# Spectral layers of a fused kernel: a second width sum built from the first, even wave numbers over d by parity, and another order of the row blocks

## The chip, the cores and the metric

The kernel runs on one core of a Trainium2 chip. Its engines are TensorE (PE in the profile, with its weight loads as PEld), VectorE (DVE), ScalarE (ACT), GpSimd (POOL) and SyncE (SP, which issues DMAs). The metric is the device time of one execution in microseconds (us); of several runs the median is given.

## The reference, cut to what matters

Two kinds of layer alternate: A (spectral filter), B (attention with 32 query heads and one key head), A, B. Sequence length is 2048, width 512, data bf16.

```python
def _A_ref(x, w_r, w_i):
    X = rfft2(x.astype(float32), axes=(-2, -1))
    return irfft2(X * (w_r + 1j * w_i), s=(S, D), axes=(-2, -1)).astype(bfloat16)

def _B_ref(x, wq, wk, wv, wo):
    q = (x @ wq).reshape(B, S, H, Dh).transpose(0, 2, 1, 3)
    k, v = x @ wk, x @ wv
    p = softmax(einsum("bhqd,bkd->bhqk", q, k) * Dh ** -0.5)
    return einsum("bhqk,bkd->bhqd", p, v).transpose(0, 2, 1, 3).reshape(B, S, H * Dh) @ wo

x = A_x
for _ in range(2):
    x = x + _A_ref(_layernorm(x), A_w_r, A_w_i)
    x = x + _B_ref(_layernorm(x), B_wq, B_wk, B_wv, B_wo)
```

## The kernel before, in words

The program is a loop over two pairs (L1010), each a spectral layer followed by an attention layer. The residual x stays in on-chip memory all the time as `x_sb`: 128 partitions, 4 row groups r, 4 blocks t, 512 columns. Transforms are matrix products with tables of sines and cosines. Sums over the sequence are split by parity into even wave numbers (block 0 of `Y`, `X4`, `SD`, `G`) and odd ones (block 1).

A spectral layer has three stages.

- **Front** (`front_first` L826, `front_next` L880): normalises the rows, forms sums and differences of rows (`butterfly` L156), and starts the sums over the sequence (`odd_sums`, matmuls at L202).
- **Middle** (`middle` L928): finishes those sums (`odd_sums`, `even_sums` L224), each followed by copies from PSUM to `Y` (`odd_out` L215, L228). `over_width` (L230) forms the product with the tables F2 over the width: for each of two real/imaginary parts, and for each part two results (index i) that differ in the sign of the sine term, 8 matmuls of 128x512 into one PSUM tile of two banks (L240, L241) and a copy by ACT (L242). `edge_sums` (L244) forms a few single columns. `filtered` (L254) multiplies by the filter `wt` and adds and subtracts on DVE (L267 and L270 for the products, L272 to L276). `over_d` (L282) transforms back over the width with table I1: 8 matmuls of 128x512 for each of 4 chunks kc (L292), and a copy by ACT to `G` (L293). `halves` (L295) adds and subtracts halves of the odd `G` on DVE (L300). In the first pair two casts of the query weights (`queries_cast` L924, copy at L925) stand in ACT's order here.
- **Blocks** (`blocks` L957): for each of the 4 blocks t, the inverse transform over the sequence, `odd(t)` (L308, copied by ACT to `bp` at L313) and `even(t, i)` (L324), both on PE. `rows_out(t)` (L326) adds and subtracts the two on DVE (L331, L332) into a tile `y` and adds `y` to the residual (L333, one operation of 128x2048). Then the next layer norm: statistics on DVE (L104, L105), a root on ACT (L108), scales on DVE (L112, L113), the rows normalised by ACT and DVE in turn (L128, L130), transposed by PE (L377), copied by ACT (L383; the last by DVE, L381), and projected to keys and values (L391, L393, L397, L400). `key_bound` (L403) reduces the keys on DVE; `first_queries` (L347) and `first_queries_cast` (L352, L356) prepare the first head group. The attention stage starts with the first score matmul (L538).

The order on PE, ACT and DVE is the order of the calls in the source: a manual schedule (L1032) keeps it, and the pools add semaphore waits where a buffer is used again. In the spectral stage the PSUM pool has three tiles of two banks (`big`, L186) and two of one bank (`bank`, L190). The tag `x4` has three buffers, `m` three, `big` in on-chip memory four. In the attention stage, which the diff leaves alone, a planner's lists fix the order; GpSimd works there on 128x512 tiles (L680) and on the normalisation of heads (L572). F2 and the other tables are loaded by SP's queue while the front runs.

Of the kernel before, what the change touches and what calls it, by code (L numbers as in the profile page):

```python
# [12 lines left out]
P = 128  # L13
# [26 lines left out]
def host_tables():  # L40
# [14 lines left out]
        f1[:, t, 4] = -f1[:, t, 3]  # L55
    tabs["F1"] = bf(f1)
    fs = (2 * p + 2, 2 * p + 1)
    f2 = np.zeros((P, 3, 2, 2, P))
    for fc in range(2):
        for c in range(2):  # L60
            a = 2 * np.pi * np.multiply.outer(128 * c + p, fs[fc]) / D
            f2[:, 0, fc, c], f2[:, 1, fc, c], f2[:, 2, fc, c] = np.cos(a), np.sin(a), -np.sin(a)
    tabs["F2"] = bf(f2)
    i1 = np.zeros((P, 3, 2, D))
    for fc in range(2):
# [88 lines left out]


def butterfly(nc, work, X, Z, bufs=3):  # L156
    s = work.tile([P, 4, 512], BF, tag="m" if bufs > 1 else "bs", bufs=bufs)
    e = work.tile([P, 4, 512], BF, tag="m" if bufs > 1 else "be", bufs=bufs)
    tt = nc.vector.tensor_tensor
    tt(out=s[:, 0:2, :], in0=X[:, 0:2, :], in1=X[:, 2:4, :], op=ALU.add)  # L160
    tt(out=e[:, 2:4, :], in0=X[:, 0:2, :], in1=X[:, 2:4, :], op=ALU.subtract)
    yield
    tt(out=e[:, 0, :], in0=s[:, 0, :], in1=s[:, 1, :], op=ALU.add)
    tt(out=e[:, 1, :], in0=s[:, 0, :], in1=s[:, 1, :], op=ALU.subtract)
    yield
    tt(out=Z[:, :, LO], in0=e[:, :, LO], in1=e[:, :, HI], op=ALU.add)  # L166
    yield
    tt(out=Z[:, :, HI], in0=e[:, :, LO], in1=e[:, :, HI], op=ALU.subtract)
    yield
# [7 lines left out]
class Spectral:  # L177


    def __init__(self, nc, tabs, work, small, psum, Z, Y, wt, w8, x_sb):  # L180
        self.nc, self.tabs, self.work, self.small, self.psum = nc, tabs, work, small, psum
        self.Z, self.Y, self.wt, self.w8, self.x_sb = Z, Y, wt, w8, x_sb
        self.pair, self.left, self.X4, self.SD, self.G, self.H, self.bp, self.pw = {}, {}, {}, {}, {}, None, {}, {}
        self.mm, self.tt = nc.tensor.matmul, nc.vector.tensor_tensor

    def big(self):  # L186
# [41 lines left out]
            self.nc.scalar.copy(out=self.Y[0][:, dc, :, 256 * q:256 * q + 256], in_=ps.rearrange("d (c k) -> d c k", c=2))  # L228

    def over_width(self, blk, fc):  # L230
        F2 = self.tabs["F2"]
        x_new = self.work.tile([P, 4, 512], BF, tag="x4", bufs=3)
        self.X4[(blk, fc)] = x_new
        for part in range(2):
            ps = self.big()
            for c in range(2):
                yr, yb = self.Y[blk][:, 2 * fc + c, 0, :], self.Y[blk][:, 2 * fc + c, 1, :]
                a, b = (yr, yb) if part == 0 else (yb, yr)
                for i, sg in enumerate((2, 1) if part == 0 else (1, 2)):
                    self.mm(ps[:, i, :], lhsT=F2[:, 0, fc, c, :], rhs=a, start=(c == 0), stop=False)  # L240
                    self.mm(ps[:, i, :], lhsT=F2[:, sg, fc, c, :], rhs=b, start=False, stop=(c == 1))  # L241
            self.nc.scalar.copy(out=x_new[:, 2 * part:2 * part + 2, :], in_=ps)  # L242

    def edge_sums(self, fc):  # L244
        F2 = self.tabs["F2"]
        pt = self.psum.tile([P, 8], F32, tag="mm", bufs=2)
        for i, (tab, q) in enumerate(((0, 0), (1, 0), (1, 1), (0, 1), (1, 0), (0, 0), (0, 1), (1, 1))):
            for c in range(2):
                self.mm(pt[:, i:i + 1], lhsT=F2[:, tab, fc, c, :], rhs=self.Y[0][:, 2 * fc + c, q, 0:1], start=(c == 0), stop=(c == 1))
        pw = self.work.tile([P, 8], F32, tag="pw", bufs=2)  # L250
        self.pw[fc] = pw
        self.tt(out=pw, in0=pt, in1=self.w8[:, fc, :], op=ALU.mult)

    def filtered(self, blk, fc):  # L254
        tt, work, wt = self.tt, self.work, self.wt
        if fc == 0:
            SD_new = work.tile([P, 2, 4, 512], BF, tag="big", bufs=4)
            self.SD[blk] = SD_new
        sd, x = self.SD[blk][:, fc, :, :], self.X4.pop((blk, fc))
        m1 = work.tile([P, 4, 512], BF, tag="m", bufs=3)  # L260
        m2 = work.tile([P, 4, 512], BF, tag="m", bufs=3)
        two = lambda a: a.rearrange("f (u v) k -> f u (v k)", u=2)
        w2 = lambda q: wt[:, fc, blk, q:q + 2, :].rearrange("f v k -> f (v k)")
        if blk == 1:
            for u in range(2):
                for m, q in ((m1, 0), (m2, 2)):
                    tt(out=two(m)[:, u, :], in0=two(x)[:, u, :], in1=w2(q), op=ALU.mult)  # L267
        else:
            for m, q in ((m1, 0), (m2, 2)):
                tt(out=two(m), in0=two(x), in1=w2(q).unsqueeze(1).broadcast_to([P, 2, 1024]), op=ALU.mult)  # L270
        uv = work.tile([P, 4, 512], BF, tag="m", bufs=3)
        tt(out=uv[:, 0:2, :], in0=m1[:, 0:2, :], in1=m2[:, 2:4, :], op=ALU.add)  # L272
        tt(out=uv[:, 2:4, :], in0=m1[:, 2:4, :], in1=m2[:, 0:2, :], op=ALU.subtract)
        u, v = (uv.rearrange("f (c w) k -> f c w k", w=2)[:, :, w, :] for w in range(2))
        tt(out=sd[:, 0:2, :], in0=u, in1=v, op=ALU.add)
        tt(out=sd[:, 2:4, :], in0=v, in1=u, op=ALU.subtract)  # L276
        if blk == 0:
            pw = self.pw.pop(fc)
            for i, slot in enumerate((0, 3, 2, 1)):
                tt(out=sd[:, slot, 0:1], in0=pw[:, i:i + 1], in1=pw[:, 4 + i:5 + i], op=ALU.add)  # L280

    def over_d(self, blk):  # L282
        I1 = self.tabs["I1"]
        G_new = self.work.tile([P, 4, 2, 512], BF, tag="big", bufs=4)
        self.G[blk] = G_new
        for kc in range(4):
            ks = slice(kc * P, (kc + 1) * P)
            ps = self.big()
            for i, terms in enumerate((((0, 0), (3, 2)), ((2, 1), (1, 0)))):
                for fc in range(2):  # L290
                    for n, (sd, tab) in enumerate(terms):
                        self.mm(ps[:, i, :], lhsT=self.SD[blk][:, fc, sd, ks], rhs=I1[:, tab, fc, :], start=(fc == 0 and n == 0), stop=(fc == 1 and n == 1))  # L292
            self.nc.scalar.copy(out=G_new[:, kc, :, :], in_=ps)  # L293

    def halves(self):  # L295

# [26 lines left out]
                tab = IE[:, 0, 2 * c + ab, t, :] if c < 2 else IE[:, 1, turned(c - 2, t, ab, i), t, :]  # L323
                self.mm(ps[:, i, :], lhsT=tab, rhs=self.G[0][:, c, ab, :], start=(c == 0 and ab == 0), stop=(c == 3 and ab == 1))  # L324

    def rows_out(self, t, parts=(slice(0, 2),)):  # L326
        ps, bp, x = self.pair.pop(t), self.bp.pop(t), self.x_sb[:, :, t, :]
        y = self.work.tile([P, 4, 512], BF, tag="m", bufs=3)
        two = y.rearrange("p (u i) d -> p u i d", u=2)
        for i in parts:  # L330
            self.tt(out=two[:, 0, i, :], in0=ps[:, i, :], in1=bp[:, i, :], op=ALU.add)  # L331
            self.tt(out=two[:, 1, i, :], in0=ps[:, i, :], in1=bp[:, i, :], op=ALU.subtract)  # L332
        self.tt(out=x, in0=y, in1=x, op=ALU.add)  # L333


class Attention:
# [18 lines left out]
    def qabs(self, qt):  # L355
        self.nc.vector.tensor_scalar(out=qt.bitcast(I16), in0=qt.bitcast(I16), scalar1=self.tabs["QAND"][:, 0:1], scalar2=None,  # L356
                                     op0=ALU.bitwise_and)
        return qt

    def stats(self, t):  # L360
        for r in range(R):
            self.norm.stats(self.x_sb[:, r, t, :], r, t)

    def scaled(self, work, t, engines):
        xn = work.tile([P, 4, 512], BF, tag="x4", bufs=3)
# [375 lines left out]
def full_kernel(ctx, tc, A_x, A_w_r, A_w_i, B_x, B_wq, B_wk, B_wv, B_wo, out, n_pairs=2):  # L741
# [186 lines left out]
    def middle(sp, first, wq_raw):  # L928
# [1 line left out]
        for dc in range(2):  # L930
            sp.odd_out(dc, (nc.scalar, nc.vector))
        sp.odd_out(2, (nc.scalar,))
        sp.over_width(1, 0)
        sp.filtered(1, 0)
        sp.odd_sums(3, range(T) if first else (T - 1,))
        sp.odd_out(3, (nc.scalar, nc.scalar))
        sp.over_width(1, 1)
        sp.filtered(1, 1)
        for dc in range(2):
            sp.even_sums(dc)  # L940
        if first:
            queries_cast(wq_raw, 0)
        sp.over_width(0, 0)
        sp.edge_sums(0)
        for dc in range(2, 4):
            sp.even_sums(dc)
        sp.filtered(0, 0)
        if first:
            queries_cast(wq_raw, 1)
        sp.over_width(0, 1)  # L950
        sp.edge_sums(1)
        sp.over_d(1)
        sp.filtered(0, 1)
        sp.halves()
        sp.over_d(0)

    def blocks(work, sp, psum, att):  # L957
# [8 lines left out]
                sp.even(t, i)  # L966

        def rows_ready(t):
            att.stats(t)
            norm.root(t)  # L970

        sp.odd(0)
        sums(0)
        sp.rows_out(0, (slice(0, 1), slice(1, 2)))
        sp.odd(1)
        sums(1)
        rows_ready(0)
        sp.odd(2)
        sums(2)
        xn = rows_scaled(0, both)  # L980
        sp.rows_out(1)
        att.transposed(psum, 0, xn)
        att.keys(psum, 0)
        rows_ready(1)
        att.key_bound(0)
        xn = rows_scaled(1, both)
        sp.odd(3)
        sums(3)
        sp.rows_out(2)
        att.transposed(psum, 1, xn)  # L990
        att.keys(psum, 1)
        att.first_queries(psum)
        rows_ready(2)
        att.key_bound(1)
        xn = rows_scaled(2, both)
        sp.rows_out(3)
        att.transposed(psum, 2, xn)
        att.keys(psum, 2)
        att.first_queries_cast()
        rows_ready(3)  # L1000
        att.key_bound(2)
        dmyo = small.tile([P, 1], F32, tag="dmyo", bufs=1)
        nc.scalar.activation(out=dmyo, in_=norm.eps, func=ACT.Exp)
        xn = rows_scaled(3, (nc.vector,) * 4)
        att.transposed(psum, 3, xn)
        att.keys(psum, 3)
        att.key_bound(3)
# [110 lines left out]
```

## Time and profile before

| what | us |
|---|---|
| median of 3 runs (1575.98 to 1577.38) | 1576.16 |
| the profiled execution | 1578.06 |
| its span | 1576.3 |
| PE busy in the span | 1357.3 (86%) |
| DVE busy | 1419.0 (90%) |
| ACT busy | 1444.8 (92%) |
| POOL busy | 796.7 (51%) |
| spectral stage of pair 0: first L240 to first L331, first L331 to first score | 38.45 to 82.71, 82.71 to 124.60 |
| the same of pair 1 | 813.17 to 855.13, 855.13 to 896.99 |

The profile shows one execution. Its times are counted from the start of the span; the device time of that execution is 1.8 us longer than the span. A row of a timeline has the start, the time from the first start to the last end of the instructions that it merges, the engine, the line, the operation, output and inputs, the shapes, the count, and in brackets the idle time before it with what ended that. Instructions on one engine overlap a little, so the distance between starts is shorter than one duration. The pairs are called pair 0 and pair 1 below, as in the code.

### The profile page before, as it was taken

How to read it: one execution, taken by the hardware profiler on the slowest of the kernel's cores; microseconds unless marked ns; L12 is line 12 of the kernel's file. 1: busy time of each engine (PE TensorE's matmuls, PEld its weight loads, DVE VectorE, ACT ScalarE, POOL GpSimd, SP SyncE). 2: the span in 40 equal slices, each digit the busy share in tenths (PEclk: the TensorE clock that was granted, in tenths of full speed). 3: DMA queues.
4: the chain of work that ended last, by engine and by line, in shares of the span. 5: the costliest groups of instructions: out<-in, count | busy, mean ns of one | idle time of the engine just before them, and what ended most of it. 6: DMA issues, size and time to landing. Idle time of an engine off the chain costs nothing.

```text
span 1576.3 us, 32981 instructions
## 1 busy us (share of the span) xinstructions
PE 1357.3 (86%) x13145; PEld 430.3 (27%) x13252; DVE 1419.0 (90%) x2261; ACT 1444.8 (92%) x1357; POOL 796.7 (51%) x1310
## 2 busy tenths in 40 slices
PE   5977888899888988898899688888998899889987
PEld 2432222222222222222234322222222222222222
DVE  7587999999999999999986889999999999999995
ACT  6658999999999999999964699999999999999996
POOL 1003565656556565665600056655556656665664
PEclk9997999999999999999999789999999999999999
DMA  8000000000000000000010000000000000000000
GB/s 270 15 1 1 2 1 1 1 1 2 1 2 1 2 1 2 1 2 1 1 41 1 0 1 2 1 2 1 5 5 5 5 5 5 5 5 5 4 5 18
DMA packets 13198, 16.95 MB, mean 11 GB/s; under 512 B 5748, under 2 KB 10484, under 8 KB 12788
## 3 DMA queue, kind: packets, MB, share of 16 engines
q1 hardware_dynamic: 12660, 13.79, 2.7%
q8 instruction: 103, 1.69, 0.4%
q0 software_dynamic: 384, 1.05, 0.2%
q14 instruction: 51, 0.42, 0.1%
HBM read 12.74 MB, written 2.10 MB: 9 GB/s over the span
## 4 chain that ended last, share of the span: by engine, by line
DVE 36%; ACT 31%; PE 14%; issue 14%; POOL 4%; DMA 0%; DVEq 0%; POOLq 0%; ACTq 0%
ACT e L627 31%; DVE t_new L661 15%; DVE s_new L676 9%; POOL pool_new L680 4%; PE pv_new L640 3%; PE sc L538 3%; DVE st L104 2%; PE new L202 2%; PE new L292 2%; DVE o L557 1%; DVE ot_new L578 1%; DVE qt L352 1%; PE dv L538 1%; PE new L241 1%; PE new L240 1%
## 5 line engine op out<-in xcount | busy, mean ns | idle before, releaser
L627 ACT ACTIVATE e<-sc 128x1536 bf16<-128x1536 f32 (+1 forms) x1158 | 1316.7, 1290 | 22.5 <-PE dv L538 18.8
L680 POOL TENSOR_SCALAR pool_new<-t_new 128x512 int16<-128x512 int16 x1204 | 748.1, 644 | 734.6 <-DVE s_new L676 648.3
L661 DVE TENSOR_SCALAR t_new<-dv 128x512 uint16<-128x512 f32 x1204 | 791.2, 677 | 76.8 <-PE dv L538 61.5
L640 PE MATMUL pv_new<-e,vaug 128*32 128x512 bf16 x2892 | 594.6, 389 | 0.0
L538 PE MATMUL sc<-qt,KT 32*128 32x512 bf16 x2892 | 458.7, 387 | 116.7 <-ACT e L627 109.4
L538 PE MATMUL dv<-qt,KT 32*128 32x512 bf16 x1204 | 454.9, 387 | 21.5 <-DVE t_new L661 19.7
L640 PE MATMUL pv_new<-s_new,vaug 128*32 128x512 bf16 x2408 | 422.8, 387 | 5.6 <-DVE s_new L676 5.6
L676 DVE TENSOR_SCALAR s_new<-t_new 128x3584 int16<-128x3584 int16 (+1 forms) x380 | 385.9, 1016 | 0.1
L640 PE MATMUL pv_new<-pool_new,vaug 128*32 128x512 bf16 x1204 | 299.2, 386 | 20.9 <-POOL pool_new L680 20.9
L538 PEld LDWEIGHTS <-KT 32*128 32x128 bf16 x4096 | 156.0, 91 | 562.9 <-issue 556.4
L640 PEld LDWEIGHTS <-vaug 128*32 128x32 bf16 x7708 | 153.8, 94 | 398.7 <-issue 367.8
L640 PE MATMUL pv_new<-t_new,vaug 128*32 128x512 bf16 x1204 | 232.1, 387 | 0.0
L347 PE MATMUL ps<-xz,wq_sb 128*128 128x512 bf16 x194 | 63.6, 385 | 4.7 <-ACT KT L393 0.6
L557 DVE STREAM_TRANSPOSE o<-pv_new 128x512 f32<-128x512 f32 x64 | 45.2, 706 | 11.1 <-PE pv_new L640 11.1
L202 PE MATMUL new<-tab_F,xz 128*128 128x512 bf16 x187 | 47.2, 402 | 3.2 <-DVE xz L166 3.0
L104 DVE BATCH_NORM_STATS2 st<-x_sb 128x6 f32<-128x512 bf16 x64 | 42.9, 670 | 3.8 <-DMA x_sb<-in_A_x_dram 3.5
L352 DVE CAST qt<-ps 128x512 bf16<-128x512 f32 x64 | 43.5, 680 | 1.2 <-PE ps L347 1.2
L572 POOL TENSOR_TENSOR od_new<-o,den 128x256 bf16<-128x256 f32 x62 | 38.4, 620 | 0.0
L347 PEld LDWEIGHTS <-wq_sb 128*128 128x128 bf16 x256 | 22.0, 97 | 32.3 <-issue 17.5
L324 PE MATMUL new<-G_new,t_new 128*128 128x512 bf16 x126 | 28.8, 379 | 0.1
L292 PE MATMUL new<-tab_I,SD_new 128*128 128x512 bf16 x124 | 27.7, 379 | 0.2
L293 ACT CAST G_new<-new 128x1024 bf16<-128x1024 f32 x16 | 16.2, 1012 | 12.2 <-PE new L292 12.2
(98 smaller groups left out, 592.7 us busy)
## 6 DMA issues: line engine op xcount, KB each, us to landing
tab_F<-const_F SPq DMA_DIRECT2D x4, 640.0 KB, 12.0
x_sb<-in_A_x_dram SPq DMA_DIRECT2D x4, 512.0 KB, 4.7
t_new<-const_IE SPq DMA_DIRECT2D x2, 1024.0 KB, 7.0
rt<-in_A_w_r_dram SPq DMA_DIRECT2D x1, 1028.0 KB, 7.2
rt<-in_A_w_i_dram SPq DMA_DIRECT2D x1, 1028.0 KB, 11.7
t_new<-const_IO SPq DMA_DIRECT2D x2, 512.0 KB, 3.4
out_dram<-x_sb SPq DMA_DIRECT2D x8, 128.0 KB, 2.0
out_dram<-x_sb POOLq DMA_DIRECT2D x8, 128.0 KB, 2.2
```

Of the source, the lines that this page charges most:

```text
L104: self.nc.vector.bn_stats(st, x_ap)
L202: self.mm(ps, lhsT=z, rhs=tab, start=start and i == 0, stop=stop and i == len(mms) - 1)
L292: self.mm(ps[:, i, :], lhsT=self.SD[blk][:, fc, sd, ks], rhs=I1[:, tab, fc, :], start=(fc == 0 and n == 0), stop=(fc == 1 and n == 1))
L347: self.nc.tensor.matmul(ps, lhsT=self.aw["wq"][:, c, hg, :], rhs=self.xT[:, c, 4 * qb:4 * qb + 4, :].rearrange("d k p -> d (k p)"), start= ...
L352: self.nc.vector.tensor_copy(out=qt, in_=ps)
L538: nc.tensor.matmul(dst, lhsT=KT[hs, kc * P:(kc + 1) * P], rhs=QT[g][hs, :], start=True, stop=True)
L557: nc.vector.transpose(out=o.rearrange("p c j -> p (c j)"), in_=ps)
L627: nc.scalar.activation(out=e[:, 0:na, :], in_=sc[:, 0:na, :], func=ACT.Exp, scale=SCALE)
L640: nc.tensor.matmul(pv[g][32 * h:32 * h + 32, :], lhsT=vaug[:, max(j, 0), kc, :], rhs=rhs, start=(first_pv[(g, h)] == u), stop=(last_pv[(g, ...
L661: nc.vector.tensor_scalar(out=tb[(g, b)][:, i, :], in0=dv, scalar1=T_MUL, scalar2=T_ADD, op0=ALU.mult, op1=ALU.add)
L676: image[0] = nc.vector.tensor_scalar(out=s_new[:, lo:nt, :], in0=src[:, lo:nt, :], scalar1=PH_OFF[i], scalar2=None, op0=ALU.add)
L680: pace(nc.gpsimd.tensor_scalar(out=sb[(g, b, 3)][:, i, :], in0=src[:, i, :], scalar1=1.0, scalar2=PH_OFF[3], op0=ALU.mult, op1=ALU.add))
```

## The change

The diff does the following.

- `over_width` uses one PSUM tile. For i = 0 it does 8 matmuls for both parts and ACT copies the result; then 4 more matmuls with twice the sines (two new tables in F2, which grows from 384 to 640 KB) are added to the same PSUM, and ACT copies again. It is a generator that yields after each copy, and `middle` puts other sums between the halves. The layout of what is copied stays the same.
- `edge_sums` copies its PSUM tile with ACT; the multiplication by `w8` moves to the end of the even `filtered`.
- `filtered` forms its products by v (four operations of 128x2x512) for both blocks.
- The even `over_d` does only the first 256 columns for each parity fc (32 matmuls of 256 columns), and DVE combines the halves into a second tile `G` (four operations).
- `rows_out` takes a number `r_add` of row groups whose residual add is done by GpSimd, one operation of 128x512 each, and DVE does the rest; it is 0 for blocks 0 and 3 and 4 for blocks 1 and 2. The order of adds and subtractions changes.
- The calls in `middle` and `blocks` stand in another order.
- `butterfly` gives its tile `s` half the size where it has one buffer.

```diff
-        for part in range(2):
-            ps = self.big()
-            for c in range(2):
-                yr, yb = self.Y[blk][:, 2 * fc + c, 0, :], self.Y[blk][:, 2 * fc + c, 1, :]
-                a, b = (yr, yb) if part == 0 else (yb, yr)
-                for i, sg in enumerate((2, 1) if part == 0 else (1, 2)):
-                    self.mm(ps[:, i, :], lhsT=F2[:, 0, fc, c, :], rhs=a, start=(c == 0), stop=False)
-                    self.mm(ps[:, i, :], lhsT=F2[:, sg, fc, c, :], rhs=b, start=False, stop=(c == 1))
-            self.nc.scalar.copy(out=x_new[:, 2 * part:2 * part + 2, :], in_=ps)
+        y = lambda c, ri: self.Y[blk][:, 2 * fc + c, ri, :]
+        for i in range(2):
+            for part in range(2):
+                for c in range(2):
+                    if i == 0:
+                        self.mm(ps[:, part, :], lhsT=F2[:, 0, fc, c, :], rhs=y(c, part), start=(c == 0), stop=False, skip_group_check=True)
+                    self.mm(ps[:, part, :], lhsT=F2[:, (2 - part, 3 + part)[i], fc, c, :], rhs=y(c, 1 - part), start=False, stop=(c == 1), skip_group_check=True)
+            self.nc.scalar.copy(out=x_new.rearrange("f (u v) k -> f u v k", v=2)[:, :, i, :], in_=ps)
+            yield
...
-        self.tt(out=pw, in0=pt, in1=self.w8[:, fc, :], op=ALU.mult)
+        self.nc.scalar.copy(out=pw, in_=pt)
...
+        for v in range(2):
             for m, q in ((m1, 0), (m2, 2)):
-                tt(out=two(m), in0=two(x), in1=w2(q).unsqueeze(1).broadcast_to([P, 2, 1024]), op=ALU.mult)
+                tt(out=uv_of(m)[:, :, v, :], in0=uv_of(x)[:, :, v, :], in1=wt[:, fc, blk, q + v, :].unsqueeze(1).broadcast_to([P, 2, 512]), op=ALU.mult)
...
+                        if split:
+                            self.mm(ps[:, i, (LO, HI)[fc]], lhsT=self.SD[blk][:, fc, sd, ks], rhs=I1[:, tab, fc, LO], start=(n == 0), stop=(n == 1))
+                        else:
+                            self.mm(ps[:, i, :], lhsT=self.SD[blk][:, fc, sd, ks], rhs=I1[:, tab, fc, :], start=(fc == 0 and n == 0), stop=(fc == 1 and n == 1))
...
+        if split:
+            G = G_new
+            G_new = self.work.tile([P, 4, 2, 512], BF, tag="big", bufs=4)
+            self.G[blk] = G_new
+            for kc in range(0, 4, 2):
+                src, dst = (a[:, kc:kc + 2, :, :].rearrange("p c a d -> p (c a) d") for a in (G, G_new))
+                self.tt(out=dst[:, :, LO], in0=src[:, :, LO], in1=src[:, :, HI], op=ALU.add)
+                self.tt(out=dst[:, :, HI], in0=src[:, :, LO], in1=src[:, :, HI], op=ALU.subtract)
...
-        for i in parts:
-            self.tt(out=two[:, 0, i, :], in0=ps[:, i, :], in1=bp[:, i, :], op=ALU.add)
-            self.tt(out=two[:, 1, i, :], in0=ps[:, i, :], in1=bp[:, i, :], op=ALU.subtract)
-        self.tt(out=x, in0=y, in1=x, op=ALU.add)
+        for u, op in enumerate((ALU.add, ALU.subtract)):
+            for i in parts:
+                self.tt(out=two[:, u, i, :], in0=ps[:, i, :], in1=bp[:, i, :], op=op)
+        for r in range(r_add):
+            self.nc.gpsimd.tensor_tensor(out=x[:, r, :], in0=y[:, r, :], in1=x[:, r, :], op=ALU.add)
+        if r_add < R:
+            self.tt(out=x[:, r_add:, :], in0=y[:, r_add:, :], in1=x[:, r_add:, :], op=ALU.add)
```

The order of the calls after the change, in `middle` (`w` is the current `over_width`, each `next(w)` one half; the queries_cast calls are in pair 0 only):

```python
w = sp.over_width(1, 0); next(w)
sp.odd_sums(3, range(T) if first else (T - 1,)); next(w)
sp.odd_out(3, (nc.scalar, nc.scalar)); sp.filtered(1, 0)
w = sp.over_width(1, 1); next(w); sp.even_sums(0); next(w); sp.filtered(1, 1)
sp.even_sums(1)
w = sp.over_width(0, 0); next(w); sp.even_sums(2); next(w); sp.edge_sums(0)
sp.even_sums(3)
w = sp.over_width(0, 1); next(w); next(w); sp.edge_sums(1)
sp.filtered(0, 0)
queries_cast(wq_raw, 0)
sp.over_d(1); sp.filtered(0, 1)
queries_cast(wq_raw, 1)
sp.halves(); sp.over_d(0)
```

and in `blocks`:

```python
sp.odd(0); sums(0); sp.rows_out(0, 0, (slice(0, 1), slice(1, 2)))
sp.odd(1); sums(1); rows_ready(0); sp.rows_out(1, R)
sp.odd(2); xn = rows_scaled(0, both); sums(2)
att.transposed(psum, 0, xn); att.keys(psum, 0)
rows_ready(1); sp.rows_out(2, R)
sp.odd(3); sums(3); xn = rows_scaled(1, both); att.key_bound(0)
att.transposed(psum, 1, xn); att.keys(psum, 1)
rows_ready(2); sp.rows_out(3, 0, (slice(0, 2),))
att.first_queries(psum); xn = rows_scaled(2, both); att.key_bound(1)
att.transposed(psum, 2, xn); att.keys(psum, 2)
rows_ready(3)
...
att.first_queries_cast(); xn = rows_scaled(3, (nc.vector,) * 4); att.key_bound(2)
att.transposed(psum, 3, xn); att.keys(psum, 3); att.key_bound(3)
```

## The prediction

> **What bounds the kernel now.** I read the 40 slices of the page first: both pairs have a long attention stage (the diff leaves its code alone) and, before it, a spectral stage at 38 to 125 us and 813 to 897 us. Then I cut each spectral stage at the places where its timeline changes hands and asked for the busy time of each engine in these windows (window, length, then busy time and count of PE, weight loads, DVE, ACT, POOL, then the PE clock):
>
> ```profile
> 38.45:82.71 44.26, 44.05 (x231) 20.52 (x234) 24.25 (x42) 27.38 (x30) 0.00 (x0) 1.00 0.07 14
> 82.71:124.60 41.89, 27.80 (x217) 15.40 (x220) 36.60 (x74) 21.08 (x42) 0.00 (x0) 0.85 0.00 1
> 813.17:855.13 41.96, 41.63 (x219) 19.33 (x222) 24.07 (x41) 23.79 (x28) 0.00 (x0) 1.00 0.00 1
> 855.13:896.99 41.86, 28.39 (x216) 15.54 (x218) 36.61 (x74) 21.08 (x42) 0.00 (x0) 0.84 0.00 1
> ```
>
> The **middle** (first L240 to first L331) is PE's: it is never idle in it. The **blocks** (first L331 to the first score matmul) are DVE's: the chain of waits stays on DVE from 82.71 to 116.84, then goes round PE, ACT and DVE to 124.60. POOL does nothing in either. So a saving counts in the middle only as PE time, in the blocks only as DVE time; PE stalls that a new order makes count in full.
>
> **The middle, what goes.** Matmuls of 512 columns follow each other every 0.2155 us (L292 below: 13.97 us for 64, of which two records are missing).
>
> ```profile
> 63.45 13.97 PE L292 MATMUL new<-tab_I,SD_new 128*128 128x512 bf16 x62
> 40.43 1.01 ACT L242 CAST x_new<-new 128x1024 bf16<-128x1024 f32 x1 [0.77 <-PE new L241]
> 60.27 1.90 ACT L925 COPY wq_sb<-wq_raw 128x2048 bf16<-128x2048 bf16 x1
> ```
>
> Four calls of `over_width` go from 16 matmuls to 12: 16 x 0.2155 = 3.45 us a pair. The even `over_d` has 32 matmuls of 256 columns instead of 512. No row has 256 columns; the nearest below is L145, 128 columns with a new weight each, four in 0.22 us in the chain of waits. I take half of 0.2155, so 3.4 us go (bounds: nothing, if 256 cost as much as 512; 5.1 us if they cost as little as 128). Together 6.85 us a pair.
>
> **The middle, what comes.** The second half of `over_width` adds to the same PSUM after the first half has been copied out. From the start of the last matmul of a half, 0.38 us to its end, 0.05 to ACT, 1.01 for L242, 0.06 back to PE: 1.5 us, less 0.22 for that matmul's own slot, leaves 1.29 us to be covered. Pair 0:
> - `over_width(0,1)` has nothing between its halves: 1.29.
> - `odd_out(3)` now stands on ACT behind the copy of the second half, so its last copy ends 0.05 + 0.90 + 0.48 + 0.59 after that half; `over_width(1,1)` can do three or four matmuls and waits: 1.6.
> - The first halves of `over_width(0,0)` and `(0,1)` need the last copy of `even_sums` straight behind it (0.38 + 0.05 + 0.59 + 0.06, less three slots): 0.43 each.
> - `queries_cast(1)` (1.90, L925) now stands on ACT ahead of the copies of the even `over_d`; PE runs out of its three PSUM buffers: 1.3.
> - The combination on DVE, four operations like L166 (0.61 apart, bf16, 128x1024), hides behind `odd(0)`; with ACT late by that cast, 0.5 shows.
>
> That is 5.6 us, so pair 0's middle gains 1.3. Pair 1 has no casts (their two rows and the 0.5 go) but only four `odd_sums` matmuls between the first halves and second halves of `over_width(1,0)`: 1.29 - 0.86 = 0.42. Sum 4.2, gain 2.7. **Both middles: -4.0 us** (bounds -2 to -6, by which stalls stand). In each even call of `filtered` four multiplies of 128x1024, 0.61 apart, take the place of two of 128x2048, 1.14 apart; DVE idles 40% of this window, so that costs nothing, and 0.3 us a pair if the cover went. F2 grows from 384 to 640 KB on SP's queue; it is issued at 24 us and lands in 4.4; L240 wants it at 38.45.
>
> **The blocks, what goes.** For t = 1 and 2 the add L333 moves from DVE to POOL, 1.24 us each: 2.5 us a pair. `key_bound(2)` (0.57) moves behind `rows_scaled(3)`, beside PE's transposes; a wait of 0.4 for the first root goes, since `rows_out(1)` now fills it. -3.5.
>
> **The blocks, what comes: POOL beside DVE.** POOL does four adds of 128x512 (two bf16 tensors) for each of the two blocks. Right behind `rows_out`, DVE's queue holds L112, L113 and two L130 of `rows_scaled`, and behind them the statistics. What happens to L130 beside POOL is in the trace, in the only place where the two meet, the end of the first attention stage:
>
> ```profile
> 90.56 0.73 DVE L130 TENSOR_SCALAR xn<-x_sb,ln_rstd,ln_nb 128x512 bf16<-128x512 bf16 x2
> 785.50 2.55 DVE L130 TENSOR_SCALAR X<-x_sb,ln_rstd,ln_nb 128x512 bf16<-128x512 bf16 x4
> 783.48 5.04 POOL L680 TENSOR_SCALAR pool_new<-t_new 128x512 int16<-128x512 int16 x7 [1.03 <-DVE s_new L676]
> 790.79 0.82 DVE L164 TENSOR_TENSOR e<-s 128x512 bf16<-128x512 bf16 x1
> L572 POOL TENSOR_TENSOR od_new<-o,den x62: 618/620/622, 158.6 to 1551.7; 128x256 bf16<-128x256 f32 x62
> ```
>
> Alone, L130 takes 0.41 us and the next starts 0.32 after; beside POOL each takes 0.69 and they follow in POOL's step of 0.62: one goes through at the end of each POOL instruction. L164 and L160, with two SBUF inputs, double or lengthen too (0.82 for 0.42; 0.97 for 0.66). L596, with one input in PSUM, stays at 0.673 to 0.679 beside POOL, and so do the statistics (L104): `rows_out`'s own adds and the statistics are safe. So I expect L113 (two SBUF inputs), L130 and L130 to wait for the second, third and fourth add, and the statistics to start when the four adds are done.
>
> The add's price p: L572 is the nearest row, 256 elements with two inputs in 0.620; POOL's 4-element operations (L121) take 0.197, so the line through both gives 1.05 at 512; twice L572 is 1.24. Below it stands L680, one input, 0.617. I take 1.10, keep 0.62 and 1.6. From the end of the first half of `rows_out` to the statistics DVE's own work is 2.0 us (1.0 left of the second half, 0.2, 0.2, 0.31, 0.31); the adds take 4 x 1.10: 2.4 us lost, twice a pair, **+4.9**.
>
> **The blocks, the tail.** `rows_out(3)` moves ahead of `rows_scaled(2)`. Before, its 3.5 us lay on DVE while PE and ACT did `transposed(2)` and `keys(2)`. Now DVE has only 5.8 us (L113, L130 twice, L403, four statistics, L352, L356) between the reciprocals of rows 2 and 3, and root(3) stands on ACT behind the copies of `keys(2)`. That round trip:
>
> ```profile
> 107.50 1.52 ACT L128 ACTIVATE xn<-x_sb,ln_nb,ln_rstd 128x512 bf16<-128x512 bf16 x2 [0.55 <-DVE ln_nb L113]
> 110.74 1.01 ACT L383 COPY xz<-ps 128x1024 bf16<-128x1024 bf16 x1 [0.69 <-PE ps L377]
> 113.60 0.58 ACT L400 ACTIVATE vaug<-psv 128x64 bf16<-128x64 f32 x4
> 112.00:116.00 4.00, 1.49 (x20) 0.86 (x18) 3.83 (x11) 1.07 (x6) 0.00 (x0) 0.55 0.00 0
> ```
>
> took 107.11 to 114.18, 7.1 us, with the clock at 1.00 until 112; with root and semaphores 7.4, so DVE would stand idle 1.6. At half clock (0.55 in this row, 0.50 after it) the transposes, keys and values take 1.9 us more: 3.5. PE will have been idle longer before it than now, but the clock held through gaps of 1.6 us before 112, so I take 3.0: **+3.0**. [...] After row 3's first L130 all runs as now (7.8 us to the first score).
>
> Blocks: -3.5 + 4.9 + 3.0 = +4.4 a pair. **Sum: -4.0 + 2 x 4.4 = +4.8 us.** The profiled execution took 1578.06 (span 1576.30 and 1.76 around it): 1582.9. The median of the runs shown, 1576.16, lies 1.9 below it; the forecast for the median is 1576.2 + 4.8 = 1581.0.
>
> **Rivals.**
> - **Adds hidden, faster.** If an add costs L680's 0.62, four take 2.5 against DVE's 2.0: 0.5 lost, not 2.4; the tail idles less, about 2.2; blocks -0.3 a pair, sum -4.6: 1571.5. The same if DVE and POOL did not exclude each other. For: POOL idle in the blocks. Against: L572, and L130 in POOL's step.
> - **One add fewer waited for, no difference.** L113 is due within 0.1 us of the first add's end. Had it slipped through, or p were over 1.19, L130 would wait for adds 2 and 3 only: 1.1 less in each of four windows, 4.4 in all, of which 0.9 goes again into the tail: 1577.5. No row has an operation as small as L113 beside POOL. [...]
> - **Slower still.** p = 1.3 to 1.6 or a stall in the middle that I missed: POOL's eight adds then hold the statistics whatever DVE does; it decides from p = 1.25 without slipping: 1584.5.
> - **The cut doesn't save.** If 256 columns cost what 512 do, 3.4 a pair come on top: 1587.8; L145 speaks against it.
>
> **Chances.** Forecast 0.48, one add fewer 0.28, hidden 0.17, the slower two 0.07. What a measurement of this kernel can tell from no change is 0.2%, 3.2 us. Forecast and the last two are slower by more, the second is within, the first is faster: 0.17 faster, 0.28 same, 0.55 slower. The range reaches from the hidden adds to p = 1.5: 1571 to 1585; the forecast's own range is 1578 to 1584.
>
> **What would show it.** In the changed profile: 12 matmuls a call with gaps of 0.4 to 1.6 us at their places, the middle at 43.0 and 39.3 us; POOL's add near 1.1 us; L113 and both L130 at about 1.1 to 1.3 beside it; the statistics of rows 1 starting 4.5 us after the first half of `rows_out(1)`; DVE idle some 3 us ahead of the reciprocal of row 3; the blocks near 46 us. It would be wrong if L130 stayed at 0.41 beside POOL, if the add took 0.6, or if the middle's stalls were not there.

## The result, and the profile after

The changed kernel takes 1579.29 us (median of 18 runs, 1577.89 to 1582.28); the kernel before takes 1576.21 (18 runs, 1574.94 to 1578.29). The ratio is 1.0021, with a 95% interval of 1.0014 to 1.0028: slower by 3.3 us, between 2.2 and 4.4. The forecast was 1581.0, slower by 4.8, in a range of 1571 to 1585.

The same windows as before, cut at the same events (first matmul of `over_width`, first operation of `rows_out`, first score matmul; columns as before: window, length, busy time and count of PE, weight loads, DVE, ACT, POOL, then the PE clock):

```profile
38.99:82.14 43.15, 38.65 (x219) 18.91 (x218) 27.00 (x50) 26.83 (x32) 0.00 (x0) 1.00 0.08 14
82.14:127.88 45.74, 31.28 (x222) 16.29 (x221) 39.14 (x72) 20.91 (x42) 9.06 (x8) 0.81 0.00 1
815.20:854.36 39.16, 36.01 (x207) 17.72 (x206) 26.90 (x49) 23.34 (x30) 0.00 (x0) 1.00 0.00 1
854.36:900.26 45.90, 32.79 (x220) 16.65 (x219) 39.13 (x72) 20.91 (x42) 9.05 (x8) 0.76 0.00 1
```

The middles became shorter by 1.11 and 2.80 us, the blocks longer by 3.85 and 4.04: together +3.98. DVE has 2.5 us more busy time in each of the blocks although 2.5 us of adds were taken from it; and PE is no longer busy all through the middle (38.65 of 43.15). The other stages are the same code, and in the twelve profiles of the table below they scatter as much as this: the first attention stage with the front behind it lies between 687.3 and 689.1 us, the second attention stage between 676.1 and 680.3. So an edit is read from its stage, and the medians only confirm the sum.

**The middle.** TensorE's timeline, pair 0 (start, length, engine, line, operation, shapes, count, and in brackets the idle time ahead with what ended it):

```profile
45.30 0.38 PE L241 MATMUL new<-y_new,tab_F 128*128 128x512 bf16 x1
46.84 0.38 PE L240 MATMUL new<-y_new,tab_F 128*128 128x512 bf16 x1 [1.16 <-ACT y_new L222]
47.33 0.38 PE L241 MATMUL new<-y_new,tab_F 128*128 128x512 bf16 x1
...
53.56 0.38 PE L240 MATMUL new<-y_new,tab_F 128*128 128x512 bf16 x1 [0.24 <-ACT y_new L228]
...
60.47 0.38 PE L240 MATMUL new<-y_new,tab_F 128*128 128x512 bf16 x1 [0.24 <-ACT y_new L228]
...
63.06 1.02 PE L241 MATMUL new<-y_new,tab_F 128*128 128x512 bf16 x4 [1.14 <-ACT x_new L242]
...
71.23 2.78 PE L291 MATMUL new<-tab_I,SD_new 128*128 128x256 bf16 x24
75.21 1.03 PE L291 MATMUL new<-tab_I,SD_new 128*128 128x256 bf16 x8 [1.19 <-ACT G_new L294]
...
79.28 2.75 PE L333 MATMUL new<-G_new,t_new 128*128 128x512 bf16 x12 [0.41 <-DVE G_new L302]
```

Each bracket is a stall that the prediction named. The idle time in the bracket counts from the end of a matmul; the price is the distance of the starts less one slot of 0.2155: at 46.84 it is 1.54 - 0.22, and 0.27 more at 47.33.

**The blocks.** DVE's timeline around the adds of block 1 and at row 3's reciprocal, first in the kernel before, then in the changed one, and POOL's in the changed one:

```profile
90.36 0.16 DVE L113 SCALAR_TENSOR_TENSOR ln_nb<-ln_mv,ln_rstd 128x4 f32<-128x4 f32 x1
...
91.21 1.22 DVE L331 TENSOR_TENSOR y<-new,bp_new 128x1024 bf16<-128x1024 f32 x1
...
94.85 0.69 DVE L104 BATCH_NORM_STATS2 st<-x_sb 128x6 f32<-128x512 bf16 x1
...
116.44 0.17 DVE L112 RECIPROCAL ln_rstd<-ln_rstd 128x4 f32<-128x4 f32 x1
```

```profile
89.13 2.34 DVE L342 TENSOR_TENSOR y<-new,bp_new 128x1024 bf16<-128x1024 f32 x2
91.38 0.17 DVE L112 RECIPROCAL ln_rstd<-ln_rstd 128x4 f32<-128x4 f32 x1
91.58 1.12 DVE L113 SCALAR_TENSOR_TENSOR ln_nb<-ln_mv,ln_rstd 128x4 f32<-128x4 f32 x1
92.74 2.36 DVE L130 TENSOR_SCALAR xn<-x_sb,ln_rstd,ln_nb 128x512 bf16<-128x512 bf16 x2
95.02 0.68 DVE L104 BATCH_NORM_STATS2 st<-x_sb 128x6 f32<-128x512 bf16 x1
...
119.75 0.18 DVE L112 RECIPROCAL ln_rstd<-ln_rstd 128x4 f32<-128x4 f32 x1 [2.44 <-ACT ln_rstd L108]
```

```profile
90.42 4.53 POOL L344 TENSOR_TENSOR x_sb<-y,x_sb 128x512 bf16<-128x512 bf16 x4 [52.80 <-DVE y L342]
```

L113 works on four elements and took 0.16 us before; here it takes 1.12. The profile counts that as busy time and shows no wait in brackets: the lengthened operation is the only sign of the exclusion in these rows. 4.53 / 4 is 1.13 us an add. Row 3's reciprocal did not wait before; now DVE is idle for 2.44 us ahead of it. This idle time is called the hole below.

### The profile page after: what moved, and what is told of

The parts are those of the page before. It is cut to its first block, busy times and chain, and to the rows that moved or that the text cites. A ratio compares the mean times of both kernels' runs of the same rounds, so it can differ in the third digit from the quotient of the medians.

```text
span 1580.5 us, 33070 instructions
## 1 busy us (share of the span) xinstructions
PE 1358.5 (86%) x13220; PEld 429.4 (27%) x13220; DVE 1430.2 (90%) x2273; ACT 1442.9 (91%) x1361; POOL 814.6 (52%) x1326
## 4 chain that ended last, share of the span: by engine, by line
DVE 35%; ACT 31%; issue 14%; PE 13%; POOL 4%; DVEq 0%; POOLq 0%; ACTq 0%
ACT e L636 30%; DVE t_new L670 16%; DVE s_new L685 9%; POOL pool_new L689 4%; PE pv_new L649 3%; PE sc L547 3%; PE new L202 1%; DVE o L566 1%; DVE ot_new L587 1%; DVE y L342 1%; DVE st L104 1%; DVE qt L365 1%; PE dv L547 1%; PE new L293 1%; PE new L241 1%
## 5 line engine op out<-in xcount | busy, mean ns | idle before, releaser
L344 POOL TENSOR_TENSOR x_sb<-y,x_sb 128x512 bf16<-128x512 bf16 x16 | 18.1, 1162 | 129.4 <-DVE y L342 129.4
L360 PE MATMUL ps<-xz,wq_sb 128*128 128x512 bf16 x256 | 67.1, 385 | 1.0 <-ACT KT L402 0.6
L266 DVE TENSOR_TENSOR m<-x_new,wt 128x1024 bf16<-128x1024 bf16 x32 | 20.7, 688 | 14.3 <-ACT x_new L242 14.3
L242 ACT CAST x_new<-new 128x1024 bf16<-128x1024 f32 x16 | 16.2, 1012 | 18.4 <-PE new L241 17.0
```

The costliest lines, as they stand in the source:

```text
L360: self.nc.tensor.matmul(ps, lhsT=self.aw["wq"][:, c, hg, :], rhs=self.xT[:, c, 4 * qb:4 * qb + 4, :].rearrange("d k p -> d (k p)"), start= ...
```

## The experiments

**The theory**: DVE's operations with two inputs in on-chip memory, and L130, do not run while a POOL add runs (in the changed kernel L113 took 1.12 us for 0.16, the two L130 1.20 and 1.24 for 0.41); one goes through at the end of each add (they begin 1.16 and 1.12 us apart, the adds 1.11); and the new block order takes the filling out of one round trip over PE and ACT. There are two windows a pair, four in all, in which POOL's adds meet DVE's `rows_scaled` and statistics. **The rivals**: the lengthening comes from shared bandwidth; or it is slack (time that would be lost anyway); or the order alone costs, and the adds on POOL are a gain; or the middle's gain is given back later. Stage times are of one profiled execution each:

| kernel | middles | blocks | median, us | ratio to the kernel before (95%) |
|---|---|---|---|---|
| before | 44.26, 41.96 | 41.89, 41.86 | 1576.21 | |
| changed | 43.15, 39.16 | 45.74, 45.90 | 1579.29 | 1.0021 (1.0014 to 1.0028) |
| e1, adds on DVE | 43.13, 39.17 | 43.37, 43.44 | 1576.82 | 0.9997 (0.9985 to 1.0008) |
| e2, POOL's adds later | 43.14, 39.17 | 44.19, 43.52 | 1575.87 | 0.9992 (0.9979 to 1.0004) |
| e3, scaling ahead of the adds | 43.15, 39.16 | 43.70, 43.78 | 1577.13 | 0.9998 (0.9987 to 1.0010) |
| e4, rows_out(3) back | 43.14, 39.16 | 44.79, 46.09 | 1579.95 | 1.0022 (1.0010 to 1.0034) |
| e5, middle alone | 43.15, 39.16 | 41.85, 41.84 | 1574.43 | 0.9986 (0.9977 to 0.9994) |
| e6, old order, adds on POOL | 43.14, 39.17 | 41.57, 41.57 | 1571.78 | 0.9974 (0.9965 to 0.9983) |
| e7, stalls covered | 39.25, 36.12 | 41.84, 41.84 | 1566.68 | 0.9945 (0.9933 to 0.9957) |
| e8, e7 and two adds on POOL | 39.25, 36.12 | 41.58, 41.58 | 1565.68 | 0.9932 (0.9919 to 0.9946) |
| e9, the rest covered | 37.67, 35.50 | 41.58, 41.57 | 1562.34 | 0.9912 (0.9897 to 0.9926) |
| e10, two adds in all blocks | 37.67, 35.50 | 41.21, 41.21 | 1561.85 | 0.9910 (0.9894 to 0.9927) |

Each group (e1 to e4, e5 to e8, e9 and e10) was measured beside its own runs of the kernel before: medians 1576.76, 1576.05 and 1576.03.

### e1: the adds on DVE again

```diff
-        sp.rows_out(1, R)
+        sp.rows_out(1, 0)
...
-        sp.rows_out(2, R)
+        sp.rows_out(2, 0)
```

> Edit: the changed kernel with the residual adds of blocks 1 and 2 on DVE again (r_add = 0), everything else as changed. Theory (DVE and POOL exclude each other): in each of the four windows DVE gets 1.24 us of add back and loses the 2.55 us that L113 and two L130 stood waiting for POOL's adds; 1.3 less a window, 5.2 in all: 1574.1. L113 at 0.16 and each L130 near 0.4; the idle time of DVE ahead of row 3's reciprocal stays (2.4). Rival (the adds on POOL are a gain, and it is the new order of the row blocks that costs): four adds of 1.24 come back to DVE and nothing goes: 1584.3. Second rival (the waits are slack, since the next root would be late anyway): no change within 1 us.

Blocks -2.37 and -2.46, together -4.8 where 5.2 was expected. DVE's timeline, with the add back in it:

```profile
91.51 1.23 DVE L346 TENSOR_TENSOR x_sb<-y,x_sb 128x2048 bf16<-128x2048 bf16 x1
92.66 0.17 DVE L112 RECIPROCAL ln_rstd<-ln_rstd 128x4 f32<-128x4 f32 x1
92.86 0.16 DVE L113 SCALAR_TENSOR_TENSOR ln_nb<-ln_mv,ln_rstd 128x4 f32<-128x4 f32 x1
93.06 0.73 DVE L130 TENSOR_SCALAR xn<-x_sb,ln_rstd,ln_nb 128x512 bf16<-128x512 bf16 x2
93.71 0.69 DVE L104 BATCH_NORM_STATS2 st<-x_sb 128x6 f32<-128x512 bf16 x1
```

L113 to the statistics takes 0.85 us here and 3.44 in the changed kernel: 2.6 us a window were waiting. More work on the bound engine made its stage shorter, so in this order neither "the adds on POOL are a gain" nor "slack" holds. The hole stays, 2.0 us in pair 0 (and 0.6 ahead of row 2's reciprocal) and 2.8 in pair 1, though POOL does no adds; the 1.5 and 1.6 us by which e1's blocks are longer than those of the kernel before are the price of the order alone.

### e2: 0.18 us more work on POOL

```diff
+        if r_add:
+            late = self.small.tile([P, 4], BF, tag="late", bufs=2)
+            self.nc.gpsimd.tensor_copy(out=late, in_=y[:, 1, 508:512])
         for r in range(r_add):
```

> Edit: one copy of 4 elements on GpSimd ahead of the four adds, so more work and every add some 0.1 to 0.2 us later. Theory (exclusion, one DVE operation goes through at the end of each add): L113 now stands at the queue's head just before the first add ends, not just after the second began (it misses by 0.03 us now); L113 takes the first gap, the two L130 the second and third, and the statistics start 0.9 us earlier; four windows: -3.7, 1575.6. Rival (DVE is slowed in proportion while POOL runs, by shared bandwidth): L113 and L130 stay as long as now, the adds end later: +0.2 to +0.8. Second rival (slack behind the waits): no change.

Blocks -1.55 and -2.38, together -3.9 (expected -3.7); the median is 3.4 lower than the changed kernel's. The pairs differ by the hole, 2.8 us in pair 0 and 2.2 in pair 1: before the transposes of row 2 PE was idle for 3.33 and 1.83 us, and its clock had fallen to 0.50 when they began in pair 0, and while they ran in pair 1. POOL's timeline, then DVE's:

```profile
90.52 0.18 POOL L345 COPY late<-y 128x4 bf16<-128x4 bf16 x1 [52.77 <-DVE y L342]
90.67 4.57 POOL L347 TENSOR_TENSOR x_sb<-y,x_sb 128x512 bf16<-128x512 bf16 x4
```

```profile
91.70 0.16 DVE L113 SCALAR_TENSOR_TENSOR ln_nb<-ln_mv,ln_rstd 128x4 f32<-128x4 f32 x1
91.90 2.34 DVE L130 TENSOR_SCALAR xn<-x_sb,ln_rstd,ln_nb 128x512 bf16<-128x512 bf16 x2
...
94.16 0.68 DVE L104 BATCH_NORM_STATS2 st<-x_sb 128x6 f32<-128x512 bf16 x1
```

In the changed kernel the second add began at 91.53 and L113 at 91.58: late by 0.05, it waited for the add's end. Here the second add begins at 91.78 and L113 at 91.70, and it takes its 0.16. The two L130 still take 1.18 and 1.24, so the bandwidth rival is out: it would have lengthened L113 as well. In these traces the order decides who waits: L113 took 0.16 us where it came first and 1.12 where it came second.

### e3: scaling ahead of the adds

```diff
+        xn = rows_scaled(0, both)
         sp.rows_out(1, R)
         sp.odd(2)
-        xn = rows_scaled(0, both)
...
+        xn = rows_scaled(1, both)
         sp.rows_out(2, R)
         sp.odd(3)
         sums(3)
-        xn = rows_scaled(1, both)
```

> Edit: rows_scaled(0) and rows_scaled(1) are called ahead of rows_out(1) and rows_out(2), so L113 and L130 run before POOL's adds begin; the adds stay on POOL. Theory: L113 at 0.16 and L130 near 0.4, DVE waits 0.4 us for the root instead; the statistics of row r then start when add r is done, 1.13 us apart (L104 itself stays near 0.67), and end about 1.0 us sooner than now in each of four windows: -4.0, 1575.3. Rival (bandwidth: POOL's adds are what is slow, whoever stands beside them): statistics start at the same time as now and the root's wait comes on top: +1.6. If POOL's adds themselves were lengthened by the DVE operations, they fall below 1.13 us here.

Blocks -2.04 and -2.12, together -4.2 (expected -4.0). DVE's timeline in block 1:

```profile
89.09 0.74 DVE L130 TENSOR_SCALAR xn<-x_sb,ln_rstd,ln_nb 128x512 bf16<-128x512 bf16 x2
...
92.23 0.69 DVE L104 BATCH_NORM_STATS2 st<-x_sb 128x6 f32<-128x512 bf16 x1
...
93.34 0.69 DVE L104 BATCH_NORM_STATS2 st<-x_sb 128x6 f32<-128x512 bf16 x1 [0.20 <-POOL x_sb L344]
```

With nothing to exclude, POOL's four adds take 4.48 (1.12 each, hardly less than 4.53), and the statistics keep their 0.69 beside them but follow in POOL's step of 1.11. So this order shows POOL's own pace as a second limit.

### e4: rows_out(3) behind rows_scaled(2) again

```diff
-        sp.rows_out(3, 0, (slice(0, 2),))
         att.first_queries(psum)
         xn = rows_scaled(2, both)
+        sp.rows_out(3, 0, (slice(0, 2),))
```

> Edit: rows_out(3) behind rows_scaled(2) again; the rest as changed. Theory (the round trip of transposed(2), keys(2) and root(3) needs rows_out(3) as DVE's filling): the 2.4 us that DVE idles ahead of row 3's reciprocal go, a wait of 0.4 for root(2) comes back: about -2.0 a pair, -4.1 in all, 1575.2. Rival (the idle time comes from TensorE's lower clock, which this order does not lift): the round trip stays as long, the idle time moves behind the first row's scaling and at most 1 us a pair goes: 1577.3 or more.

This expectation failed: blocks -0.95 and +0.19, and the median is within 0.7 us of the changed kernel's. DVE's timeline, pair 0 and then pair 1:

```profile
109.35 0.18 DVE L112 RECIPROCAL ln_rstd<-ln_rstd 128x4 f32<-128x4 f32 x1 [1.47 <-ACT ln_rstd L108]
...
118.69 0.17 DVE L112 RECIPROCAL ln_rstd<-ln_rstd 128x4 f32<-128x4 f32 x1
```

```profile
882.84 0.18 DVE L112 RECIPROCAL ln_rstd<-ln_rstd 128x4 f32<-128x4 f32 x1 [2.78 <-ACT ln_rstd L108]
```

The hole ahead of row 3's reciprocal is gone, and a new one stands ahead of row 2's. The reason is in the order as a whole. From the scaling of row t, DVE must wait for transposes, keys and root(t+1). The old order puts `rows_out(t+1)` into every one of these round trips; the changed one has put each `rows_out` one trip earlier, so one trip is left without, and moving only the last call moves the hole. In pair 1 it costs more: PE, at a clock of 0.50 from 868 to 874, is still at the sums of block 3 until 877.9, 1.6 us after the last L130. So the rival that blamed TensorE's clock has a share there, but hardly in pair 0, where the transposes began 0.3 us behind L130.

### e5 and e6: the old order, without and with POOL

Both take the changed kernel's middle and the calls of `blocks` in the order of before. In e5 all adds are on DVE; e6 is

```diff
-        sp.rows_out(1, 0)
+        sp.rows_out(1, R)
...
-        sp.rows_out(2, 0)
+        sp.rows_out(2, R)
```

> Edit: the changed kernel's middle with the block order of the kernel before, all residual adds on DVE. Theory (middle and blocks are separate, and the whole loss is in the blocks): middle 43.1 and 39.2 us as in the changed kernel, blocks 41.9 twice as in the kernel before, -3.9 against the kernel before: 1572.3. Rival (the gain of the middle is given back later, because DVE or ACT come late into the blocks): blocks over 42.5, time within 2 us of the kernel before.

> Edit: as e5, but the adds of blocks 1 and 2 on POOL (r_add = R), behind rows_scaled of the block ahead as in the order of before. Theory: the order of the calls makes the hole in the tail, POOL's adds make the waits. Here L113 and L130 run before the adds begin, and the hole has rows_out(3) in it again; but the statistics follow the adds 1.13 us apart, 4 x 1.13 + 0.85 = 5.4 us from the first half to the last statistics against 1.0 + 1.24 + 3.2 = 5.4 with DVE's own add. So blocks 41.9 as in e5, the POOL adds gain nothing: 1572.3. Rival (in an order without clashes the adds on POOL do gain the 1.24 us each): blocks 39.4, 1567.3. Rival of the other sign (the hole is made by the adds, not by the order): blocks over 43, 1575 or more.

e5 has the blocks of before to 0.04 us, and the middles of the changed kernel: the two parts are separate, and nothing of the middle's gain is given back. (By the ratio e5 is faster than the kernel before by 2.2 us, 0.9 to 3.6, where the stages say 4.0. No stage that the edit touches explains the rest, and it stays open.) e6 shows blocks of 41.57, so POOL's adds without a clash gain 0.28 a pair, not 2.5. They make the statistics follow in POOL's step:

```profile
93.97 0.69 DVE L104 BATCH_NORM_STATS2 st<-x_sb 128x6 f32<-128x512 bf16 x1 [0.20 <-POOL x_sb L344]
...
95.08 0.69 DVE L104 BATCH_NORM_STATS2 st<-x_sb 128x6 f32<-128x512 bf16 x1 [0.20 <-POOL x_sb L344]
```

e6 has no hole, with the adds on POOL; e1 has it, with the adds on DVE. That settles e4: the order makes the hole, the adds do not.

### e7 to e10: a version that beats both

e7 covers the middle's stalls by order alone (against e5; `over_d` takes the chunks kc that it is to do):

```diff
-        sp.odd_sums(3, range(T) if first else (T - 1,)); next(w)
-        sp.odd_out(3, (nc.scalar, nc.scalar)); sp.filtered(1, 0)
-        w = sp.over_width(1, 1); next(w); sp.even_sums(0); next(w); sp.filtered(1, 1)
-        sp.even_sums(1)
+        sp.odd_sums(3, range(T) if first else (T - 1,))
+        sp.odd_out(3, (nc.scalar, nc.vector)); next(w); sp.filtered(1, 0)
+        w = sp.over_width(1, 1); next(w); sp.even_sums(0); sp.even_sums(1); next(w); sp.filtered(1, 1)
+        if first: queries_cast(wq_raw, 0)
-        w = sp.over_width(0, 0); next(w); sp.even_sums(2); next(w); sp.edge_sums(0)
-        sp.even_sums(3)
-        w = sp.over_width(0, 1); next(w); next(w); sp.edge_sums(1)
+        w = sp.over_width(0, 0); next(w); sp.even_sums(2); sp.even_sums(3); next(w); sp.edge_sums(0)
+        w = sp.over_width(0, 1); next(w); sp.over_d(1, (0,)); next(w); sp.edge_sums(1)
         sp.filtered(0, 0)
-        queries_cast(wq_raw, 0)
-        sp.over_d(1); sp.filtered(0, 1)
-        queries_cast(wq_raw, 1)
+        if first: queries_cast(wq_raw, 1)
+        sp.over_d(1, (1, 2, 3)); sp.filtered(0, 1)
```

> Edit: as e5, and the middle's PE stalls covered by order alone: odd_out(3) ahead of the second half with one copy on DVE, both even_sums of a pair ahead of the second half, the first chunk of the odd over_d between the halves of over_width(0,1), queries_cast where ACT idles. Theory (the middle is bound by PE and the stalls of 5.6 and 4.2 us are all that hides the cut of 6.85): middle 37.4 and 35.1, blocks as e5, 1576.2 - 13.7 = 1562.5. Rival (ACT or DVE is next behind PE by less than that: 27 of 43 us busy, but in chains of copies): some stalls come back elsewhere, middle 39 to 41 and 37 to 38, 1566 to 1570.

Middles 39.25 and 36.12: the rival's range in pair 0, between theory and rival in pair 1; the median is in the rival's range. Two stalls were left, in pair 0's PE timeline (the second in both pairs):

```profile
54.96 1.89 PE L202 MATMUL new<-tab_F,xz 128*128 128x512 bf16 x8 [0.84 <-ACT y_new L228]
...
68.69 3.45 PE L293 MATMUL new<-tab_I,SD_new 128*128 128x256 bf16 x30 [0.46 <-DVE SD_new L277]
```

e8 adds `r_add = 2` in blocks 1 and 2, and takes the statistics in the order of rows 0, 2, 3, 1:

```diff
-            for r in range(R):
+            for r in ((0, 2, 3, 1) if t in (1, 2) else range(R)):
...
-        sp.rows_out(1, 0)
+        sp.rows_out(1, 2)
...
-        sp.rows_out(2, 0)
+        sp.rows_out(2, 2)
```

> Edit: as e7, with two of the four row groups of blocks 1 and 2 added by POOL (r_add = 2) and the statistics taken in the order of rows 0, 2, 3, 1. Theory (exclusion: DVE's add of two rows waits for the end of POOL's first add, POOL's second add then runs beside the statistics, which do not exclude it): 1.0 + 0.15 + 0.62 + 3.2 = 5.0 us from the first half of rows_out to the last statistics against 5.4: -0.44 in four windows, -1.8 against e7: 1560.7. Rival (POOL's second add starts late or is pushed on by further DVE operations, and the statistics wait): no gain, or up to +1.1 a window.

Blocks -0.26 each, not -0.88. POOL, then DVE, in e8:

```profile
87.94 2.78 POOL L346 TENSOR_TENSOR x_sb<-y,x_sb 128x512 bf16<-128x512 bf16 x2 [50.43 <-DVE y L344]
```

```profile
89.01 0.69 DVE L348 TENSOR_TENSOR x_sb<-y,x_sb 128x1024 bf16<-128x1024 bf16 x1
...
101.59 0.69 DVE L414 TENSOR_REDUCE kmax<-KT 128x1 f32<-128x512 bf16 x1 [0.87 <-ACT KT L404]
```

DVE's add of two rows came when the first POOL add was ending, took its 0.69, and now POOL's second add waited for it: two adds took 2.78 where 2.26 would be two of 1.13. The windows did become shorter, by 0.65 us each (0.44 was expected); but in the second one DVE then met `key_bound(1)` 0.87 us ahead of the copy of the keys that it reads. The round trip over PE and ACT is the next limit.

e9 moves two calls in the middle (below, against e8); e10 takes `r_add = 2` and the new order of the statistics in all four blocks:

```diff
         sp.odd_sums(3, range(T) if first else (T - 1,))
+        if first:
+            queries_cast(wq_raw, 0)
...
         sp.filtered(1, 1)
-        if first:
-            queries_cast(wq_raw, 0)
...
-        sp.even_sums(2); sp.even_sums(3); next(w); sp.edge_sums(0)
+        sp.even_sums(2); next(w); sp.even_sums(3); sp.edge_sums(0)
```

> Edit: as e8, with the two stalls that e7's middle still shows covered: queries_cast(0) goes ahead of odd_out(3), where ACT idled 2.0 us, instead of ahead of the copies that even_sums(2) waits for (0.84 us of PE, pair 0 only), and the second half of over_width(0,0) goes ahead of even_sums(3), so that DVE gets it 1.7 us sooner and filtered(0,1) is done before the even over_d wants it (0.46 us of PE, both pairs). Theory: middle 37.9 and 35.7 (39.25 and 36.12 in e7), blocks 41.6 as in e8, so -1.8 against e8. Rival (the copies of even_sums(3) come late instead, as in the changed kernel): 0.43 less of that in each pair, -0.9.

> Edit: as e9, with r_add = 2 in all four blocks. Theory (DVE is the bound of the blocks up to row 3's reciprocal, so each block in which POOL takes two row groups gives 0.6): blocks 40.4, -2.4 against e9. Rival (e8 gave 0.26 of 1.2, because DVE then waited for ACT's copy of keys(1), 0.87 us: the round trip over PE and ACT is next): the block 0 share is lost in that wait, the block 3 share alone counts: blocks 41.0, -1.2.

e9's middle and blocks in pair 0, by engine:

```profile
37.97:75.64 37.67, 37.66 (x219) 18.91 (x218) 27.33 (x50) 26.26 (x31) 0.00 (x0) 1.00 0.09 17
75.64:117.22 41.58, 28.59 (x221) 15.52 (x220) 35.52 (x74) 20.93 (x42) 5.57 (x4) 0.85 0.00 1
```

PE is busy 37.66 of 37.67 us again: bound by PE, with no stall left, and both middles are shorter than before, by 6.59 and 6.46 us where the cut was reckoned as 6.85. e10's blocks are 0.37 shorter, less than the rival's 0.6:

```profile
78.98 1.07 DVE L348 TENSOR_TENSOR x_sb<-y,x_sb 128x1024 bf16<-128x1024 bf16 x1
...
105.34 0.53 DVE L371 TENSOR_SCALAR qt<-qt,tab_QAND 128x512 int16<-128x512 int16 x1
```

In block 0 DVE's own add came while a POOL add ran and took 1.07 us for the 0.69 that it takes in e8 (in blocks 1 and 2); what was left of that block's gain went into the wait at `key_bound(1)`, which grew to 1.08. In block 3 the add's step was 0.54 us shorter, but L371, beside POOL's second add, took 0.53 us where it takes 0.35 in e8. e9 and e10 can't be told apart by their medians; both are faster than the kernel before by 0.9%, 14 us.

## Why the prediction was right, step by step

- **A cut counts in the middle only as PE time.** Right: e9 brought 6.5 of the 6.85. A matmul of 256 columns was taken as half of 0.2155; in pair 1 the even `over_d` and the next matmul begin at 845.24 and 848.73, 0.109 us for each of the 32.
- **PE stalls of 5.6 and 4.2.** Right, one by one (pair 0): `odd_out(3)` 1.6 (said 1.6), the copies of `even_sums` 0.40 each (0.43), the halves of `over_width(0,1)` 1.30 (1.29), the cast ahead of the copies 1.4 (1.3), the combination 0.6 (0.5). Middles 43.15 and 39.16, said 43.0 and 39.3.
- **Blocks -3.5.** A little too small, it is -3.8. `rows_out(1)` took DVE 3.64 us before (91.21 to 94.85) and takes 2.25 in the changed kernel (89.13 to 91.38): the add and the gap ahead of it are worth 1.39 us, not 1.24. Twice that, with the 0.57 and the 0.4, is 3.75; with the next two terms as measured (5.2 and 2.4, in pair 1 2.6) it gives +3.9 and +4.1, where the blocks show 3.85 and 4.04.
- **POOL beside DVE, +4.9.** Right: 1.13 us an add (said 1.10; the upper bound of 1.6 was the author's, no row of the kernel before shows it), L113 1.12, the L130 in steps of 1.12 and 1.16, the statistics 4.6 us after the first half of `rows_out(1)` (said 4.5), 2.6 us lost a window (said 2.4); 5.2 a pair. The rival that L113 slips through missed by 0.05 us, and e2 made it true: 3.9 us in all, where the rival was priced at 3.5 below the forecast. The rows of the kernel before could not decide between the two, as the prediction says itself (within 0.1 us); that it fell on the forecast's side was luck.
- **The tail, +3.0.** The mechanism was right, the size was the term most off: DVE idled 2.44 us (2.6 in pair 1), and from row 3's L130 to the first score it took 7.7, as before. From reciprocal to reciprocal the round trip took 8.3 us where 8.8 was reckoned (7.4, and 1.4 for the clock): the clock halved only between the two halves of the transposes of row 2, of which eight took 0.62 us and the next eight 1.01. The 3.0 was the author's choice between 1.6 at full and 3.5 at half clock; PE's longest gap there was 2.80 (1.47 in pair 1), and behind it the clock fell from 1.00 to 0.50 in both pairs. The size is not a fixed one: in the four kernels with this order at the tail (the changed one, e1 to e3) the hole was between 2.0 and 2.9 us.
- **F2's larger transfer at no cost.** No delay is seen: the first L240 stands at 38.99 in the changed kernel and between 37.9 and 39.1 in the ten kernels with the same tables, at 38.45 before.
- **Sum.** Said -4.0 + 8.8; measured in the stages -3.9 + 7.9 = +4.0, and +3.3 in the ratio of the runs, whose interval (2.2 to 4.4) holds the 4.0 but not the 4.8. The misses in the sum partly cancel, which is luck too: -0.3 by the adds that went and +0.3 by those that came, a pair, and the tail 0.4 to 0.6 too long. What lies between the two is within the scatter of the attention stages and was not followed up.

What the prediction did not see is how the hole belongs to the order: it named `rows_out(3)` as the one call that moved, and the undoing of that call alone (e4) moved the hole and gained 0.95 us in one pair and nothing in the other.

## What to carry to other kernels

Work given to POOL was not free here where a DVE operation with two inputs in on-chip memory (L113, 1.12 us for 0.16), or the TENSOR_SCALAR L130 (1.20 and 1.24 for 0.41), came due while it ran: 2.6 us lost a window. Where only the statistics ran beside it, four adds gained little, since the statistics followed in POOL's step of 1.11 us (e6, 0.28 us a pair); two adds of four shortened a window by 0.65 (e8). Look for such operations in DVE's queue right behind the producer, and for operations of known length that have grown, since no wait is shown. Saved PE time is worth what its copies let through (of a cut of 6.85 us the changed kernel's middles kept 1.11 and 2.80, e9's 6.59 and 6.46): put independent matmuls between a result and the matmul that needs its copy, and read each gap by start distances. When a filling operation moves ahead by one round trip, count the trips that have none left before undoing a single call.

## What the runs showed of the hardware that was not expected

- POOL and DVE hold each other up in both directions: POOL's second add took 1.67 us in e8 behind a DVE add, and an add took 1.14 to 1.20 in the changed kernel; a DVE add of 0.69 us took 1.07 in e10's block 0.
- The PE clock fell to 0.50 in the middle of the blocks of the changed kernel (below; columns as in the windows above) after gaps of 1.28, 0.39 and 1.10 us, with 1.5 us of matmuls between 92.4 and 96.65. The gaps do not decide it alone: e2 has the same ones in both pairs (0.32, 0.36 and 1.10 us, the middle one 0.37 in pair 1), and there the clock held 1.00 in pair 0 and fell to 0.50 in pair 1; why is open. DVE was the bound there, so it cost nothing that the stages show, except in e4's pair 1.

```profile
95.00:96.00 1.00, 0.40 (x4) 0.32 (x5) 0.97 (x4) 0.85 (x2) 0.00 (x0) 1.00 0.00 0
96.00:97.00 1.00, 0.35 (x2) 0.15 (x2) 0.96 (x3) 0.60 (x1) 0.00 (x0) 0.89 0.00 0
97.00:98.00 1.00, 1.00 (x4) 0.41 (x3) 0.96 (x3) 0.00 (x0) 0.00 (x0) 0.50 0.00 0
```
